# Storing K in one DRAM tensor so that a block is reloaded with its halo, putting one block's Q chunks ahead of its K chunks and moving one VectorE step earlier, in a two-layer attention and gated-MLP kernel

## The chip, the cores and the metric

The kernel runs on one core of one Trainium2 chip. The metric is device time in microseconds (us). The first three timed runs of the kernel before gave a median of 1631.23 us (1631.12 to 1631.37). Every execution also reports its span (first to last instruction), which is about 1.7 us shorter than its time, and the mean clock granted to TensorE. In the traces PE is TensorE's matmuls, PEld its weight loads, DVE VectorE, ACT ScalarE, POOL GpSimd, and SPq the SyncE queue, which issues nearly all DMAs (transfers), in program order. A DMA lands when its data has arrived. PSUM is the memory that TensorE writes its results to. Matmuls are called cold where the granted clock is low: a group of 8 takes 1.73 us at full clock.

## The reference

Two layers share one set of weights. Each is a sliding, dilated attention and a ReLU-gated MLP, each behind a layer norm and added to the residual. S = 2048 tokens, D = 1024, 32 heads of 32, MLP width 3584.

```python
qkv = (x @ wqkv).reshape(B, S, 3, H, Dh)          # ... split into q, k, v
idx = pos[:, None] - (arange(8) * 2)[None, :]     # 8 keys per query: 0, 2, ..., 14 tokens back
logits = einsum("bhsd,bhswd->bhsw", q, kg) * scale     # kg: k gathered at idx; -1e9 where idx < 0
o = einsum("bhsw,bhswd->bhsd", softmax(logits), vg)
x = x + o @ wo
gate, up = xn @ W_gate, xn @ W_up                 # xn = layernorm(x)
x = x + ((gate * (gate > 0)) * up) @ W_down
```

The keys of a query reach 14 tokens back. So a block of 512 tokens needs the last 14 K columns of the block before it: its halo.

## The kernel before

The tokens go through in four blocks of 512, twice (numbers 0 to 3 for layer one, 4 to 7 for layer two). TensorE makes V, Q, K, output projection, gate/up and down products; VectorE multiplies Q by the eight shifted Ks and sums over chunks (`t`, `ac`, `s`), and TensorE sums `s` over each head (`head_mm`, tile `L`). In layer one, Q and K of blocks 1 to 3 are made early, cast by ScalarE into a small staging pool (six buffers), stored to DRAM, and reloaded when VectorE gets to them. That is where the change is.

The halo was built on chip: each staged K chunk was widened by 14 columns that GpSimd copied in from the block before, and GpSimd saved its own last 14 columns for the block after.

```python
def f_(nm, c):                       # one chunk c of Q or K of block n: 8 matmuls, one cast
    def f():
        if nm == "k" and c == 0:
            khalo[n] = qk_pool.tile([P, KC, HALO], BF16, tag="kh", name=f"kh_{n}", bufs=2)
        ...                          # 8 matmuls into a PSUM buffer "acc" (six of them)
        else:
            k = tile_of("k", c, HALO + BLK)
            tail_act[0] = nc.scalar.copy(k[:, HALO:HALO + BLK], acc[:]).ins
            if b == 0:
                nc.gpsimd.memset(k[:, 0:HALO], 0.0)
            else:
                nc.gpsimd.tensor_copy(k[:, 0:HALO], khalo[n - 1][:, c, :])
            nc.gpsimd.tensor_copy(khalo[n][:, c, :], k[:, BLK:BLK + HALO])
    return f

QK_FIRST = [(nm, c) for c in range(KC) for nm in ("q", "k")]     # q0 k0 q1 k1 ...
```

The weights come in 1 MB slabs through a ring of five buffers; a slab's load is put into the queue at the time when a buffer should come free, and the author states when each slab was used last (`want_qk`: Q slabs, K slabs). The order of all instructions is fixed by a list of events with planned times, in units of `GRP` = 1.73 us, the time of one group of 8 matmuls:

```python
want_qk("qk01", t_v1, t_v1)          # both Q and K slabs of blocks 0 and 1 held until V of block 1 starts
want_v("v123", ...)                  # two V slabs; the second takes over a Q slab's buffer
...
qk1, puts1, gets1 = qk_steps(1, ln_a[1], "qk01", True)
ev.append((t_v2 + 2.2 * GRP, lambda: head_mm(0)))
...
spread(puts[ahead:], t_fill + GRP + 1.2, GRP)      # last K stores of blocks 2 and 3
spread(sums1[4:6], t_wo0 + 1.0, 6.0)               # products and sums of block 1
...
t_head1 = t_gu0 + 37.0
ev.append((t_head1, lambda: head_mm(1)))
ev.append((t_gu0 - 0.01, start_hidden))            # closes the staging pool, opens the MLP's hidden pool
```

`start_hidden` matters: the MLP's tiles (`r`, the ReLU of a gate, and `hT`) take over the memory of the staging pool. The first ReLU can therefore not start before the last staged K chunk has been read out by its store.

Of the kernel before, what the change touches and what calls it, by code (L numbers as in the profile page):

```python
# [7 lines left out]
BF16 = mybir.dt.bfloat16  # L8
# [5 lines left out]
P = 128  # L14
# [5 lines left out]
HALO = (W - 1) * DIL  # L20
KC = D // P
BLK = 512
# [14 lines left out]
def kernel(  # L37
# [11 lines left out]
    nc = tc.nc  # L49
    S = A_x.shape[1]  # L50
    F = B_W_gate.shape[1]
    assert A_x.shape[2] == D and S % BLK == 0 and F % P == 0
    NB = S // BLK
# [19 lines left out]
    dram = ctx.enter_context(tc.tile_pool(name="dram", bufs=1, space=bass.MemoryType.DRAM))  # L73
# [4 lines left out]
    qk_pool = ctx.enter_context(tc.tile_pool(name="qk", bufs=KC))  # L78
# [5 lines left out]
    pool = {}  # L84
# [25 lines left out]
    tail_act = [None]  # L110
# [4 lines left out]
    def sp_dma(dst, src, transpose=False):  # L115
        start = nc.sync.dma_start_transpose if transpose else nc.sync.dma_start
        if tail_sp[0] is None:
            tail_sp[0] = start(dst, src).ins
        else:
            with tc.issue_after(tail_sp[0]):  # L120
                tail_sp[0] = start(dst, src).ins  # L121

    @contextmanager
    def pe_group():
        if tail_pe[0] is None:
            yield
        else:
            with tc.issue_after(tail_pe[0]):
                yield

    def mm(*args, **kwargs):
        tail_pe[0] = nc.tensor.matmul(*args, **kwargs).ins  # L132
# [24 lines left out]
    NTOK = HALO + S  # L157
    v_d = dram.tile([H * DH, NTOK], BF16, name="v_d")
    o_d = dram.tile([NT, H, DH, P], BF16, name="o_d")
    q_d = [dram.tile([KC, P, BLK], BF16, name=f"q_d{n}") for n in range(1, NB)]  # L160
    k_d = [dram.tile([KC, P, HALO + BLK], BF16, name=f"k_d{n}") for n in range(1, NB)]
    s_d = [dram.tile([P, W * BLK], BF16, name=f"s_d{i}") for i in range(2)]
    zpad = const.tile([P, KC, HALO], BF16, name="zpad")
    nc.gpsimd.memset(zpad[:], 0.0)
# [22 lines left out]
    def want(key, src, use_end):  # L187
        slab_plan.append((key, src, use_end))

    def want_v(key, mid, end):  # L190
        for g in range(2):
            want((key, g), wqkv_v[:, :, 2 * D + g * SLAB:2 * D + (g + 1) * SLAB], mid if g == 0 else end)

    def want_qk(key, q_end, k_end):
        for i, (nm, end) in enumerate((("q", q_end), ("k", k_end))):
            for hh in range(2):
                want((key, nm, hh), wqkv_v[:, hh * (KC // 2):(hh + 1) * (KC // 2), i * D:(i + 1) * D], end)
# [242 lines left out]
    def store_v(n):  # L440
        def f():
            dst = bass.AP(tensor=v_d.tensor, offset=v_d.offset + HALO + (n % NB) * BLK,
                          ap=[[NTOK, P], [P * NTOK, KC], [1, BLK]])
            sp_dma(dst, att[n]["vT"][:])
        return f

    khalo = {}
# [8 lines left out]
    def qk_steps(n, ln, key, staged=False):  # L456
        b = n % NB
        st = att[n]
        staging = {}

        def tile_of(nm, c, cols):
            if staged:
                t = pool["stage"].tile([P, HALO + BLK], BF16, tag="st", name=f"{nm}st_{n}_{c}")
                staging[nm, c] = t[:, 0:cols]
                return t[:, 0:cols]
            t = qk_pool.tile([P, cols], BF16, tag=nm, name=f"{nm}_{n}_{c}")
            st[(nm, c)] = t
            return t[:]

        def f_(nm, c):  # L470
            def f():
                if nm == "k" and c == 0:
                    khalo[n] = qk_pool.tile([P, KC, HALO], BF16, tag="kh", name=f"kh_{n}", bufs=2)
                acc = psum.tile([P, BLK], F32, tag="acc", name=f"acc_{nm}")
                with pe_group():
                    for kc in range(KC):
                        w = slab[(key, nm, kc // (KC // 2))][:, kc % (KC // 2), bass.ds(c, P, KC)]
                        mm(acc[:], lhsT=w, rhs=ln["xnT"][:, :, kc, :], start=(kc == 0), stop=(kc == KC - 1))
                if nm == "q":
                    q = tile_of("q", c, BLK)  # L480
                    tail_act[0] = nc.scalar.copy(q, acc[:]).ins
                else:
                    k = tile_of("k", c, HALO + BLK)
                    tail_act[0] = nc.scalar.copy(k[:, HALO:HALO + BLK], acc[:]).ins  # L484
# [6 lines that stand above are left out]

        def put(nm, c):
            def f():
                sp_dma((q_d if nm == "q" else k_d)[n - 1][c], staging.pop((nm, c)))
            return f

        def get(nm, c):
            def f():
                t = qk_pool.tile([P, BLK if nm == "q" else HALO + BLK], BF16, tag=nm, name=f"{nm}_{n}_{c}")
                st[(nm, c)] = t  # L500
                sp_dma(t[:], (q_d if nm == "q" else k_d)[n - 1][c])
            return f

        order = QK_FIRST if n < NB else QK_ORDER
        steps = [f_(nm, c) for nm, c in order]
        if not staged:
            return steps
        return steps, [put(nm, c) for nm, c in order], [get(nm, c) for nm, c in order]

    def head_mm(n):  # L510
        st = att[n]
        st["L"] = psum_l.tile([P, W, P], F32, tag="L", name=f"L_{n}")
        with pe_group():
            for wh in range(2):
                for tq in range(TPB):
                    mm(st["L"][32 * tq:32 * tq + 32, WH * wh:WH * (wh + 1), :], lhsT=sel[:],
                       rhs=st["s"][:, WH * wh:WH * (wh + 1), tq * P:(tq + 1) * P],
                       start=True, stop=True, skip_group_check=True, tile_position=(0, 32 * tq))
# [281 lines left out]
    GRP = 1.73  # L800
# [4 lines left out]
    def spread(steps, at, gap):  # L805
        for i, f in enumerate(steps):
            ev.append((at + gap * i, f))

    ev = []
    ln_a = {}  # L810
# [6 lines left out]
    def ln1(n, at, turn_at, early=False, gap=3.0, dve=()):  # L817
        stats, apply, turn, hold = ln_steps(n, "a", early, dve)
        ln_a[n] = hold
        spread(stats, at, gap)  # L820
        spread(apply, at + (2 * gap if dve else max(3 * gap, 12.0)), gap)
        ev.append((turn_at, turn()))
# [15 lines left out]
    t_qk1 = t_qk0 + GRP * 2 * KC  # L838
    t_v1 = t_qk1 + GRP * 2 * KC
    t_v2 = t_v1 + GRP * KC  # L840
    t_v3 = t_v2 + GRP * KC
    t_qk2 = t_v3 + GRP * KC
    ahead = 2 * KC + 6
    t_wo0 = t_qk2 + GRP * ahead
# [1 line left out]
    t_gu0 = t_fill + GRP * (4 * KC - ahead)  # L846

    want_v("v0", t_v0 + GRP * 5, t_qk0)
    want_qk("qk01", t_v1, t_v1)
    want_v("v123", t_v3 + GRP * KC / 2, t_qk2)  # L850
    want_qk("qk23", t_qk2 + GRP * 2 * KC, t_gu0)
    want_wo(0, t_fill, t_fill)
# [10 lines left out]
    ev.append((t_qk0 + 4.0, store_v(0)))  # L863
    ev.append((t_qk0 + 18.0, lambda: load_x(3)))
    spread(qk_steps(0, ln_a[0], "qk01"), t_qk0, GRP)
    spread(prod_sum_steps(0), t_qk0 + 3.5, 4.4)
    spread(load_v_steps(0), t_qk0 + 19.0, 1.0)
    ln1(2, t_qk0 + 10.0, t_qk1 + 10.5, True, 4.5)
    qk1, puts1, gets1 = qk_steps(1, ln_a[1], "qk01", True)
    spread(qk1, t_qk1, GRP)  # L870
    spread(puts1, t_qk1 + GRP + 1.2, GRP)
    ln1(3, t_qk1 + 10.0, t_v2 + 0.4, True, 5.0)
    spread(v_steps(1, ln_a[1], "v123", True), t_v1, GRP)
# [9 lines left out]
    ev.append((t_v3 + 3.0, store_v(2)))  # L883
    spread(v_steps(3, ln_a[3], "v123", True), t_v3, GRP)
    ev.append((t_qk2 + 3.0, store_v(3)))
    spread(gets1, t_v3 + 4.0, 1.6)
    qk2, puts2, gets2 = qk_steps(2, ln_a[2], "qk23", True)
    qk3, puts3, gets3 = qk_steps(3, ln_a[3], "qk23", True)
    steps = qk2[0::2] + qk3[0::2] + qk2[1::2] + qk3[1::2]
# [7 lines left out]
    ln2(0, wo_ats, 3.0, [wo_ats[-1] + 1.0 + 1.3 * t for t in range(TPB)], (1, 2, 3))  # L897
    sums1 = prod_sum_steps(1)
    spread(sums1[:4], t_pv0 + 34.5, 4.5)
    spread(sums1[4:6], t_wo0 + 1.0, 6.0)  # L900
    spread(sums1[6:10], t_fill + 1.4, 4.6)
    spread(sums1[10:], t_gu0 + 2.6, 5.4)
    spread(load_v_steps(1), t_wo0 + 4.0, 7.0)
# [97 lines left out]
```

## Time and profile before

| | kernel before |
|---|---|
| time, first timed runs | 1631.23 us |
| the profiled execution: time, span | 1632.73 us, 1631.0 us |
| PE busy | 1612.0 us of the span |
| first wait of PE: V weights | 2.16 us at 87 us |
| second wait of PE: first ReLU | 7.36 us at 206 us |

The first line of the profile's page for the kernel before: busy time, share of the span and instructions of each engine.

```profile
PE 1612.0 (99%) x7513; PEld 784.8 (48%) x7562; DVE 1135.3 (70%) x961; ACT 476.5 (29%) x971; POOL 228.5 (14%) x212
```

TensorE leaves 19 us idle: 9.5 in the two waits above, 3.9 in the first 10 us of the program, 3.0 in its last 3 us, the rest in small pieces. Nothing can be won but what TensorE waits, and the slow matmuls that follow a wait. The table of waits of the kernel before (engine, what waited, for what: us in total, times, longest):

```profile
PE acc_g L132 <- ACT r L722: 7.4, 1, 7.4
...
DVE L L106 <- PE L L132: 3.4, 1, 3.4
...
PE acc_v L132 <- DMA w_v<-in_A_wqkv_dram: 3.0, 2, 2.2
```

The first line is the large stall, the last the small one (2.2 of its 3.0 us).

The small stall, from the timeline of the kernel before (start, duration, engine, line, operation, operands, count, and in brackets the idle time before it and what ended it):

```profile
80.00 7.07 PE L132 MATMUL acc_v<-xnT_a,w_v 128*128 128x512 bf16 x32
...
83.20 0.38 SPq L121 DMA_DIRECT2D w_v<-in_A_wqkv_dram  x1
...
89.23 5.96 PE L132 MATMUL acc_v<-xnT_a,w_v 128*128 128x512 bf16 x19 [2.16 <-DMA w_v<-in_A_wqkv_dram]
```

And from its chain of waits (start, duration, what):

```profile
80.05 2.21 POOL kst L488
...
82.28 0.32 SPq L121
```

The second V slab's buffer was free at 80.0, but the queue reached its load at 83.20, behind K stores that waited for GpSimd (its copy ended at 82.26, the store went at 82.28).

The large stall, from the same kernel's timeline:

```profile
194.51 8.05 SPq L121 DMA_DIRECT2D k_d<-kst  x4
...
196.03 0.59 ACT L484 CAST kst<-acc_k 128x512 bf16<-128x512 f32 x1 [0.91 <-DMA k_d<-kst]
...
199.88 4.48 DVE L106 TENSOR_TENSOR t<-q,k 128x2048 f32<-128x2048 bf16 x2
199.95 4.46 POOL L488 COPY kst<-kh 128x14 bf16<-128x14 bf16 x2
...
202.99 0.83 SPq L121 DMA_DIRECT2D w_u<-in_B_W_up_dram  x1
...
203.93 0.52 SPq L121 DMA_DIRECT2D w_g<-in_B_W_gate_dram  x1
...
204.55 1.66 SPq L121 DMA_DIRECT2D k_d<-kst  x1
...
212.41 1.57 ACT L722 ACTIVATE r<-acc_g 128x512 bf16<-128x512 f32 x3 [15.80 <-DMA k_d<-kst]
...
213.06 3.54 PE L132 MATMUL acc_g<-xnT_b,w_g 128*128 128x512 bf16 x8 [7.36 <-ACT r L722]
```

The last K chunk was cast by 196.6, but two GpSimd copies of 14 columns took 4.46 us, exactly beside two VectorE instructions of 4.48 us. The Trainium skill ("SBUF — State Buffer", section "SBUF: two separate sides") says that GpSimd and VectorE share a port pair into SBUF, the on-chip memory, as an exclusive lock, held for a whole instruction, and that a VectorE instruction with two inputs in SBUF, as these products have, contends for it with a GpSimd instruction that reads SBUF; this trace agrees: such a copy took 189 ns at its fastest and about 2.26 us beside VectorE's 2.28 us products. Only then could the store be issued, behind two 1 MB weight loads, and it landed about 8 us later. After it came the first ReLU.

Busy time of each engine in two stretches around the stalls, kernel before, with granted clock (PEclk), DMA share and GB/s:

```profile
80.00:100.00 20.00, 17.84 (x76) 7.56 (x75) 19.86 (x9) 12.06 (x26) 9.51 (x7) 0.91 0.70 244
200.00:225.00 25.00, 17.64 (x75) 7.58 (x74) 18.52 (x13) 3.37 (x6) 6.75 (x5) 0.86 0.56 180
```

Columns after the length: PE, PEld, DVE, ACT, POOL. A clock below 1.00 marks time at a lowered rate, which can begin during a wait (0.50 from 210 to 213 us, where no matmul ran) and goes on into the matmuls after it.

### The profile page before, as it was taken

The page shows a single profiled execution, that of the slowest core. Times are in us where ns is not written, and L with a number is a line of the kernel's source. Part 1 is how long each engine was busy: PE and PEld are TensorE (multiplying, and loading weights), DVE is VectorE, ACT ScalarE, POOL GpSimd, SP SyncE. Part 2 cuts the span into 40 slices and gives each one's busy share as a digit, 9 for nine tenths or more (in the row PEclk, how much of TensorE's full clock was granted, in tenths as well). Part 3 has the DMA queues.
Part 4 walks back from the last instruction along what each step waited for, and adds up shares of the span by engine and source line. Part 5 has one row for each costly group of instructions (what it writes and reads, how often), then busy time and mean ns, then how long its engine had stood idle before and what let it go on. Part 6 is the DMA issues. An engine that isn't in the chain of part 4 may idle for free.

```text
span 1631.0 us, 18776 instructions
## 1 busy us (share of the span) xinstructions
PE 1612.0 (99%) x7513; PEld 784.8 (48%) x7562; DVE 1135.3 (70%) x961; ACT 476.5 (29%) x971; POOL 228.5 (14%) x212
## 2 busy tenths in 40 slices
PE   9999989999999999999999999999999999999999
PEld 6646534444444445444454444544445444444444
DVE  6989889895979699939579295792948929311211
ACT  4843212041107222523135131360313301131110
POOL 2613500010003002210052000530005100000000
PEclk9999999999999999999999999999999999999999
DMA  9668756779579776785846948579585795655452
GB/s 294 139 207 250 174 168 197 209 186 241 185 208 212 174 216 190 200 222 166 232 159 186 229 154 230 181 184 251 167 225 161 204 251 162 207 156 179 155 162 71
DMA packets 401655, 315.87 MB, mean 194 GB/s; under 512 B 161056, under 2 KB 383648, under 8 KB 399904
## 3 DMA queue, kind: packets, MB, share of 16 engines
q1 hardware_dynamic: 400992, 314.09, 68.1%
q8 instruction: 59, 0.97, 0.3%
q10 hardware_dynamic: 576, 0.59, 0.1%
q14 instruction: 28, 0.23, 0.0%
HBM read 265.24 MB, written 33.67 MB: 183 GB/s over the span
## 4 chain that ended last, share of the span: by engine, by line
PE 97%; DMA 1%; issue 0%; POOL 0%; ACT 0%; SPq 0%; DVE 0%; DVEq 0%; ACTq 0%; POOLq 0%
PE acc_g L132 24%; PE acc_u L132 24%; PE dacc L132 18%; PE acc_wo L132 7%; PE acc_v L132 6%; PE acc_q L132 6%; PE acc_k L132 6%; PE dacc_pair L132 6%; DMA w_v<-in_A_wqkv_dram 1%; DMA k_d<-kst 1%; POOL st_a L249 0%; POOL kst L488 0%; SPq L121 0%; ACT xn_a L245 0%; PE L L132 0%
## 5 line engine op out<-in xcount | busy, mean ns | idle before, releaser
L132 PE MATMUL acc_g<-xnT_b,w_g 128*128 128x512 bf16 x1792 | 425.0, 380 | 7.4 <-ACT r L722 7.4
L132 PE MATMUL acc_u<-xnT_b,w_u 128*128 128x512 bf16 x1792 | 423.3, 379 | 0.0
L722 ACT ACTIVATE r<-acc_g 128x512 bf16<-128x512 f32 x224 | 133.4, 597 | 734.6 <-PE acc_g L132 663.0
L106 DVE TENSOR_TENSOR hT<-acc_u,r 128x512 bf16<-128x512 f32 x224 | 150.7, 686 | 245.6 <-PE acc_u L132 236.6
L132 PE MATMUL dacc<-w_d,hT 128*128 128x512 bf16 (+1 forms) x1372 | 300.4, 375 | 1.5
L132 PEld LDWEIGHTS <-w_g 128*128 128x128 bf16 x1792 | 175.6, 98 | 220.0 <-issue 9.7
L132 PEld LDWEIGHTS <-hT 128*128 128x128 bf16 x1820 | 178.1, 98 | 208.9
L132 PEld LDWEIGHTS <-w_u 128*128 128x128 bf16 x1792 | 175.4, 98 | 211.8 <-issue 0.5
L106 DVE TENSOR_TENSOR pv<-a,vhm 128x4096 bf16<-128x4096 bf16 x64 | 143.5, 2282 | 0.0
L541 DVE TENSOR_TENSOR t<-q,k 128x2048 f32<-128x2048 bf16 x56 | 128.0, 2291 | 6.7 <-ACT k L484 4.6
L769 DVE TENSOR_TENSOR x<-dacc,x 128x512 bf16<-128x512 f32 (+1 forms) x38 | 24.5, 672 | 154.2 <-PE dacc L132 154.2
L106 DVE TENSOR_TENSOR t<-q,k 128x2048 f32<-128x2048 bf16 x56 | 127.5, 2287 | 4.0 <-ACT k L484 2.4
L489 POOL COPY kh<-k 128x14 bf16<-128x14 bf16 x40 | 53.7, 1348 | 511.1 <-ACT k L484 511.1
L106 DVE TENSOR_TENSOR pv<-pv 128x1024 bf16<-128x1024 bf16 (+1 forms) x128 | 113.6, 948 | 0.0
L249 POOL TENSOR_TENSOR st_b<-st_b,neg_half 128x1 f32<-128x1 f32 x29 | 39.5, 1369 | 520.3 <-ACT st_b L248 520.3
L132 PE MATMUL acc_wo<-w_o,oT 128*128 128x512 bf16 x498 | 111.1, 379 | 0.7
L554 DVE TENSOR_TENSOR ac<-ac,t 128x2048 f32<-128x2048 f32 x48 | 109.6, 2283 | 0.3
L106 DVE TENSOR_TENSOR ac<-ac,t 128x2048 f32<-128x2048 f32 x48 | 109.6, 2283 | 0.0
L132 PE MATMUL dacc_pair<-w_d,hT 128*128 128x512 bf16 x413 | 95.5, 379 | 0.4
L132 PEld LDWEIGHTS <-oT 128*128 128x128 bf16 x512 | 50.0, 98 | 60.4
L244 ACT ACTIVATE xn_b<-x 128x1024 bf16<-128x1024 bf16 x29 | 30.3, 1046 | 124.2 <-DVE x L695 62.1
L410 ACT CAST vT<-acc_v 128x512 bf16<-128x512 f32 x56 | 32.7, 584 | 60.5 <-PE acc_v L132 60.5
(133 smaller groups left out, 1285.1 us busy)
## 6 DMA issues: line engine op xcount, KB each, us to landing
w_g<-in_B_W_gate_dram SPq DMA_DIRECT2D x56, 1024.0 KB, 6.7
w_u<-in_B_W_up_dram SPq DMA_DIRECT2D x56, 1024.0 KB, 5.3
w_d<-in_B_W_down_dram SPq DMA_DIRECT2D x48, 1024.0 KB, 5.9
w_o<-in_A_wo_dram SPq DMA_DIRECT2D x16, 1024.0 KB, 7.3
vhm<-v_d SPq DMA_DIRECT2D x32, 284.0 KB, 6.7
v_d<-vT SPq DMA_DIRECT2D x8, 1024.0 KB, 9.4
oT<-o_d SPq DMA_DIRECT2D x32, 256.0 KB, 4.2
w_d<-in_B_W_down_dram SPq DMA_DIRECT2D x16, 512.0 KB, 3.7
```

What stands on the lines that cost most here:

```text
L106: tail_dve[0] = f(*args, **kwargs).ins
L132: tail_pe[0] = nc.tensor.matmul(*args, **kwargs).ins
L244: nc.scalar.activation(xn, xt[:], ACT.Square, accum_out=sq)
L249: nc.gpsimd.tensor_tensor(rstd, vpe, neg_half[:, 0:1], op=ALU.pow)
L410: tail_act[0] = nc.scalar.copy(st["vT"][:, c, :], acc[:]).ins
L489: nc.gpsimd.tensor_copy(khalo[n][:, c, :], k[:, BLK:BLK + HALO])
L541: nc.vector.tensor_tensor(t[:], i0, i1, op=ALU.mult)
L554: nc.vector.tensor_tensor(o, ac[:], t[:], op=ALU.add)
L722: tail_act[0] = nc.scalar.activation(rs[j][:], acc[:], ACT.Relu).ins
L769: run = dv if n < NB - 2 else (lambda f, *args, **kwargs: f(*args, **kwargs))
```

## The change

K is stored once, without halo, into one DRAM tensor of all tokens, so that a block can be reloaded together with the 14 columns ahead of it: the widened read replaces 48 GpSimd copies. Block 0, which is never staged, keeps its copies, and one small store puts its last 14 columns into that tensor. For block 1 all Q chunks go ahead of all K chunks, so that the Q slabs come free 8 groups earlier. One step of block 1's products and sums moves 3.5 us earlier.

```diff
-    q_d = [dram.tile([KC, P, BLK], BF16, name=f"q_d{n}") for n in range(1, NB)]
-    k_d = [dram.tile([KC, P, HALO + BLK], BF16, name=f"k_d{n}") for n in range(1, NB)]
+    q_d = dram.tile([KC, P, S], BF16, name="q_d")
+    k_d = dram.tile([KC, P, S], BF16, name="k_d")
 ... (staging tiles are now 512 wide; khalo only where not staged)
+                elif staged:
+                    tail_act[0] = nc.scalar.copy(tile_of("k", c, BLK), acc[:]).ins
                 else:
                     k = tile_of("k", c, HALO + BLK)
 ... (put: stores to columns b*BLK to (b+1)*BLK)
 def get(nm, c):
-                sp_dma(t[:], (q_d if nm == "q" else k_d)[n - 1][c])
+                sp_dma(t[:], (q_d if nm == "q" else k_d)[c, :, b * BLK - lead:(b + 1) * BLK])   # lead: 14 for K
+    def store_halo(n):
+            end = (n % NB + 1) * BLK
+            sp_dma(k_d[:, :, end - HALO:end].rearrange("c p t -> p c t"), khalo[n][:])
 ...
-    want_qk("qk01", t_v1, t_v1)
+    want_qk("qk01", t_qk1 + GRP * KC, t_v1)
 ...
-    qk1, puts1, gets1 = qk_steps(1, ln_a[1], "qk01", True)
+    qk1, puts1, gets1 = (part[0::2] + part[1::2] for part in qk_steps(1, ln_a[1], "qk01", True))
+    ev.append((t_qk1 + 9.0, store_halo(0)))
 ... (block 1's reloads still alternate q and k)
-    spread(sums1[4:6], t_wo0 + 1.0, 6.0)
+    spread(sums1[4:6], t_wo0 + 1.0, 2.5)
```

More of the change, by code (lines that the diff above doesn't have):

```diff
@@ L462, in tile_of @@
             if staged:
-                t = pool["stage"].tile([P, HALO + BLK], BF16, tag="st", name=f"{nm}st_{n}_{c}")
-                staging[nm, c] = t[:, 0:cols]
-                return t[:, 0:cols]
+                staging[nm, c] = pool["stage"].tile([P, BLK], BF16, tag="st", name=f"{nm}st_{n}_{c}")
+                return staging[nm, c][:]
             t = qk_pool.tile([P, cols], BF16, tag=nm, name=f"{nm}_{n}_{c}")
@@ L471, in f @@
             def f():
-                if nm == "k" and c == 0:
+                if nm == "k" and c == 0 and not staged:
                     khalo[n] = qk_pool.tile([P, KC, HALO], BF16, tag="kh", name=f"kh_{n}", bufs=2)
@@ L493, in f @@
             def f():
-                sp_dma((q_d if nm == "q" else k_d)[n - 1][c], staging.pop((nm, c)))
+                sp_dma((q_d if nm == "q" else k_d)[c, :, b * BLK:(b + 1) * BLK], staging.pop((nm, c))[:])
             return f
@@ L498, in f @@
             def f():
-                t = qk_pool.tile([P, BLK if nm == "q" else HALO + BLK], BF16, tag=nm, name=f"{nm}_{n}_{c}")
+                lead = 0 if nm == "q" else HALO
+                t = qk_pool.tile([P, lead + BLK], BF16, tag=nm, name=f"{nm}_{n}_{c}")
                 st[(nm, c)] = t
-                sp_dma(t[:], (q_d if nm == "q" else k_d)[n - 1][c])
+                sp_dma(t[:], (q_d if nm == "q" else k_d)[c, :, b * BLK - lead:(b + 1) * BLK])
             return f
@@ L508, in qk_steps, with f @@
         return steps, [put(nm, c) for nm, c in order], [get(nm, c) for nm, c in order]
+    def store_halo(n):
+        def f():
+            end = (n % NB + 1) * BLK
+            sp_dma(k_d[:, :, end - HALO:end].rearrange("c p t -> p c t"), khalo[n][:])
+        return f
     def head_mm(n):
@@ L885 @@
     ev.append((t_qk2 + 3.0, store_v(3)))
-    spread(gets1, t_v3 + 4.0, 1.6)
+    spread([f for pair in zip(gets1[:KC], gets1[KC:]) for f in pair], t_v3 + 4.0, 1.6)
     qk2, puts2, gets2 = qk_steps(2, ln_a[2], "qk23", True)
```

## The prediction

> **What bounds the kernel.** TensorE: the page's busy table gives PE 1612.0 of 1631.0 us; the chain that ended last is 97% PE. The table of waits shows two stalls worth removing:
>
> 1. 87.07 to 89.23 us: value projection waits 2.16 us for the second slab of V weights. The timeline shows its load issued only at 83.20. Its slot in the ring comes free when the last K chunk of block 1 ends (80.0), and the issuing queue stood behind K stores waiting for GpSimd halo copies.
> 2. 205.70 to 213.06 us: six PSUM buffers are full because the first ReLU waits for the last K store to land (chain of waits: DMA k_d<-kst 7.71 us, then ACT r); the hidden-layer pool takes over the staging memory. That store was issued at 204.55, though its cast ended at 196.6. GpSimd copies of 14 columns took 189 ns when free but about 2.26 us, one DVE operation, when DVE was busy; the queue sat 194.51 to 202.56 in four K stores, and two weight loads of 1 MB went ahead of the last store.
>
> Each stall also chills TensorE[...]: 8 matmuls after stall 2 took 3.54 us where 1.73 is usual, +1.81; 19 after stall 1 took 5.96 against 4.10, +1.86. The windows show granted clock 0.84 and 0.91 there. Together 2.16 + 1.86 + 7.36 + 1.81 = 13.2 us. Start (about 10 us) and tail (about 3) are untouched.
>
> **What changes.** 48 GpSimd copies go (windows by tile: 58 us of GpSimd), so staged K stores wait for ACT alone. One store of 1024 pieces of 28 bytes comes; the like store of zeros landed in 8.3 us, and this one has tens of us before its first reader. With Q first, the Q slabs of block 1 free at about 66 us, so the V slab is issued some 17 us earlier and lands near 75, needed at 87. Moving one product/sum step 3.5 us earlier lets DVE fill about 2 us of idle time between the residual adds at 166 to 171 us.
>
> **On the critical path.** Stall 1 goes: -4.0 us. Stall 2: two weight loads and the last store can issue at about 195.5 to 196.8 (old time scale) instead of 202.99 to 204.55. First load to landing took 9.3 us, so the store lands near 204.8, the first ReLU ends near 205.4, and PE needs its buffer at 205.70. DVE, which ran to 206.56 before the first gate, is about 2 us earlier; the first up buffer is needed at 207.4. So the stall nearly closes, by a small margin: I give back 0.3 of 9.17. Sum 4.0 + 8.9 = 12.9; 1631.2 - 12.9 = 1618.3; with small new waits **1618.6 us**, range 1617.0 to 1622.5. Faster by over 2%: 0.005; within 2%: 0.985; slower: 0.01.
>
> **What would show it.** No PE wait for w_v; that slab's load issued near 66. No copies onto kst, GpSimd busy down about 58 us. Last K store issued about 9 us before the sixth gate/up group ends; PE wait for r from 7.4 to under 1 us. PE busy down about 3.7 us (no cold matmuls). No new PE wait.
>
> **What would make it wrong.** The last store lands 1 to 3 us later behind the weights: a short stall that brings back the cold 1.8 us (about 1621). Stores into one shared DRAM tensor ordered against reloads of other blocks, stalling the issuing queue. The small-piece store delaying Q stores until staging runs out. Early Q slab loads crowding stores and so ACT. DVE, with less slack in the first gate/up stage, holding PSUM.

## More of the kernel before

Note that the profiled execution was 1.5 us longer than the timed ones.

The head sums of block 0 in the kernel before, from the timeline:

```profile
103.11 0.61 PE L132 MATMUL L<-s,sel 128*32 128x512 bf16 x8
...
103.66 1.69 PE L132 MATMUL acc_v<-xnT_a,w_v 128*128 128x512 bf16 x7
103.78 0.27 DVE L106 TENSOR_TENSOR L<-L,maskc 32x112 f32<-32x112 f32 x1 [3.43 <-PE L L132]
```

VectorE had finished at 103.78 - 3.43 = 100.35, so TensorE, arriving at 103.11, found its data there with 2.8 us to spare. The head sums of block 1, from the same kernel's timeline:

```profile
239.97 2.29 DVE L106 TENSOR_TENSOR s<-ac,t 128x2048 bf16<-128x2048 f32 x1
...
242.43 0.61 PE L132 MATMUL L<-s,sel 128*32 128x512 bf16 x8
```

Here VectorE finished at 242.26, 0.17 us before TensorE came.

## The result, and the profile after

| | before | after |
|---|---|---|
| time, median (lowest to highest) | 1631.30 us (1631.12 to 1631.68) | 1622.68 us (1622.30 to 1623.05) |
| ratio of fast runs, 95% interval | | 0.9947 (0.9930 to 0.9964) |
| span of the profiled execution | 1631.0 us | 1620.6 us |
| PE waits for V weights at 87 us | 2.16 us | none |
| PE wait for the first ReLU | 7.36 us | 0.20 us |
| PE waits for `s` at the head sums | none | 0.84 and 1.14 us |

A ratio is the mean time of one kernel's fast runs over the mean of the other's in the same rounds, so it is not quite the ratio of the medians. The record marks an execution slow when it is over 1.5% above the fastest of the same kernel; none was. The change is 0.5% faster, 8.6 us; 12.6 were forecast (1631.2 to 1618.6), and 1622.68 lies just outside the forecast range (1617.0 to 1622.5).

Page of the kernel after, busy time:

```profile
PE 1609.6 (99%) x7513; PEld 784.4 (48%) x7562; DVE 1135.1 (70%) x961; ACT 475.8 (29%) x971; POOL 174.1 (11%) x164
```

48 GpSimd instructions and 54.4 us of its busy time are gone; PE is busy 2.4 us less for the same matmuls, where 3.7 were forecast: the windows from the V projection to block 0's head sums and from the first to the eighth gate/up group lost 1.86 and 1.62 us of busy time, but the first 20 us gained 0.62, and the two split head sums about 0.2 each. Table of PE's waits, kernel after:

```profile
PE L L132 <- DVE s L106: 2.0, 2, 1.1
...
PE acc_v L132 <- DMA w_v<-in_A_wqkv_dram: 1.0, 1, 1.0
...
PE acc_g L132 <- ACT r L730: 0.2, 1, 0.2
```

Both old stalls are gone (the w_v line that is left is at the start of the program, 10 us). In their place stands a wait that was not in the table of before: head sums wait for VectorE. The small stall, kernel after:

```profile
72.05 0.40 SPq L121 DMA_DIRECT2D w_v<-in_A_wqkv_dram  x1
...
80.08 19.16 PE L132 MATMUL acc_v<-xnT_a,w_v 128*128 128x512 bf16 x88
```

Now the slab's load is issued 11 us earlier, and 88 matmuls run without a gap. Timeline of the kernel after, at the hand-over from staging to hidden pool:

```profile
191.83 0.39 SPq L121 DMA_DIRECT2D w_u<-in_B_W_up_dram  x1
...
192.46 0.46 SPq L121 DMA_DIRECT2D w_g<-in_B_W_gate_dram  x1
...
192.51 0.59 ACT L482 CAST kst<-acc_k 128x512 bf16<-128x512 f32 x1 [1.14 <-PE acc_k L132]
193.12 2.93 SPq L121 DMA_DIRECT2D k_d<-kst  x1
...
202.34 1.57 ACT L730 ACTIVATE r<-acc_g 128x512 bf16<-128x512 f32 x3 [9.25 <-DMA k_d<-kst]
...
202.99 1.89 PE L132 MATMUL acc_g<-xnT_b,w_g 128*128 128x512 bf16 x8 [0.20 <-ACT r L730]
```

The store now follows its cast at once (193.12 against 192.51 + 0.59). It still takes 9 us to land, behind the weights, but the six PSUM buffers hide that to within 0.20 us.

The head sums of block 0, kernel after:

```profile
98.06 2.29 DVE L106 TENSOR_TENSOR s<-ac,t 128x2048 bf16<-128x2048 f32 x1
99.17 0.40 PE L132 MATMUL L<-s,sel 128*32 128x512 bf16 x4
...
100.41 0.40 PE L132 MATMUL L<-s,sel 128*32 128x512 bf16 x4 [0.84 <-DVE s L106]
...
100.74 1.47 PE L132 MATMUL acc_v<-xnT_a,w_v 128*128 128x512 bf16 x6
```

VectorE writes `s` at 98.06 to 100.35, to the hundredth where it did before. TensorE arrives 3.94 us earlier than before. The 2.8 us to spare have become a wait. The group took 100.74 - 99.17 = 1.57 us where before the next started after 103.66 - 103.11 = 0.55: 1.02 us lost. The head sums of block 1, kernel after:

```profile
229.90 2.29 DVE L106 TENSOR_TENSOR s<-ac,t 128x2048 bf16<-128x2048 f32 x1
...
230.70 0.40 PE L132 MATMUL L<-s,sel 128*32 128x512 bf16 x4
...
232.24 0.40 PE L132 MATMUL L<-s,sel 128*32 128x512 bf16 x4 [1.14 <-DVE s L106]
...
232.57 1.69 PE L132 MATMUL acc_g<-xnT_b,w_g 128*128 128x512 bf16 x7
```

Here the group took 232.57 - 230.70 = 1.87 us against 0.55: 1.32 us lost. The stretches shown of before, in the kernel after:

```profile
80.00:100.00 20.00, 19.57 (x94) 8.63 (x92) 19.86 (x9) 15.18 (x30) 1.63 (x2) 1.00 0.63 193
200.00:225.00 25.00, 24.80 (x116) 11.16 (x114) 23.39 (x17) 5.16 (x9) 0.00 (x0) 1.00 0.51 162
```

The clock is back at 1.00; VectorE's share of the second stretch rose from 18.5 to 23.4 us.

Added up from the starts of the same groups in both traces: the first gate group starts 2.92 us earlier (195.18 to 192.26), the eighth gate/up group 11.72 us earlier (216.43 to 204.71), so the large stall gave 8.80 us; the second head sums took 1.32 back; 11.72 - 1.32 = 10.4, the difference of the spans.

### The profile page after: what moved, and what is told of

Same layout as the page of the kernel before. It is cut to its first block, busy times and chain, and to the rows that moved or that the text cites. A ratio compares the mean times of both kernels' runs of the same rounds, so it can differ in the third digit from the quotient of the medians.

```text
span 1620.6 us, 18710 instructions
## 1 busy us (share of the span) xinstructions
PE 1609.6 (99%) x7513; PEld 784.4 (48%) x7562; DVE 1135.1 (70%) x961; ACT 475.8 (29%) x971; POOL 174.1 (11%) x164
## 4 chain that ended last, share of the span: by engine, by line
PE 93%; DVE 4%; DMA 1%; issue 1%; ACT 0%; SPq 0%; DVEq 0%; POOL 0%; ACTq 0%
PE acc_g L132 23%; PE acc_u L132 23%; PE dacc L132 18%; PE acc_wo L132 7%; PE acc_k L132 6%; PE acc_q L132 6%; PE acc_v L132 6%; PE dacc_pair L132 6%; DVE ac L106 2%; DVE t L106 2%; DMA k_d<-kst 1%; DMA w_v<-in_A_wqkv_dram 0%; DVE s L106 0%; DVE hT L106 0%; ACT xn_a L263 0%
```

## The experiments

Each was one kernel of before or after with an edit. All were correct. "Before" in a row is the kernel before, run in the same rounds on the same chip; its level differs by up to 1.6 us from chip to chip, so the ratios and the traces are compared. Times are medians.

| run | time | before | ratio (95%) | span of the profile | PE waits: V slab, ReLU, head sums |
|---|---|---|---|---|---|
| b_again | 1632.70 | 1632.84 | 1.0002 (0.9989 to 1.0015) | 1631.0 | 2.20, 7.66, none |
| b_kdram | 1625.55 | 1632.84 | 0.9960 (0.9948 to 0.9973) | 1623.8 | none, 2.93, 0.83 |
| b_qfirst | 1630.41 | 1632.84 | 0.9988 (0.9975 to 1.0002) | 1628.6 | none, 8.08, 0.87 |
| b_put | 1625.75 | 1632.84 | 0.9958 (0.9946 to 0.9971) | 1624.4 | 2.44, 2.29, none |
| after_again | 1622.14 | 1631.25 | 0.9943 (0.9930 to 0.9955) | 1620.4 | none, none, 0.83 + 1.14 |
| a_noq | 1622.24 | 1631.25 | 0.9942 (0.9930 to 0.9955) | 1620.7 | none, 0.9, 0.82 + 1.14 |
| a_sums | 1625.15 | 1632.24 | 0.9961 (0.9947 to 0.9975) | 1623.7 | none, 2.99, 0.82 |
| a_put | 1620.55 | 1631.25 | 0.9933 (0.9920 to 0.9945) | 1618.9 | none, none, 0.83 |
| a_head01 | 1620.08 | 1631.25 | 0.9931 (0.9917 to 0.9944) | 1617.9 | none, none, none |
| a_best | 1619.37 | 1632.24 | 0.9922 (0.9910 to 0.9935) | 1617.3 | none, none, none |

By the 2% rule every one counts as "same" as before; the intervals, and the waits above all, are what tells them apart.

The theory after the result: the two stalls went as forecast, and the missing gain is in two places: 2.3 us of new waits at the head sums, and about 1.5 us that were never there in the timed runs, because the profile was of a longer execution. Rivals: that the profile itself lengthens an execution; that VectorE limits the whole stage, so that moving a wait moves nothing; and, on the parts of the change, that the order of Q and K is what did it.

### The kernel before, unchanged (b_again, b_look1, b_look2)

> The kernel before, unchanged. The prediction took 13.2 us of stall from one profile whose execution took 1632.73 us, 1.5 us more than the 1631.2 us of the timed ones. Theory A (the profile on record caught longer stalls than usual): timed spans near 1629.6, and a second profile shows the wait before acc_v below 2.16 us or the wait before acc_g below 7.36 us, together 1 to 2 us less idle or cold time on TensorE. Rival B (profiling itself adds 1.5 us to any execution): the second profile is again near 1631.0 of span with the same two waits, and the timed spans of this run are near 1629.6 all the same.

Its profile has span 1631.0 again with the same two waits, but so had its timed runs (1630.6 to 1632.5), and profiled and unprofiled ones mix. So rival B falls: profiling adds nothing that shows. The kernel before just scatters: in all its runs here, spans from 1628.6 to 1633.0. Theory A's means, a shorter wait, was not seen either. What differs showed in two more looks.

> The kernel before, unchanged, one more profile. Both profiles so far have span 1631.0 and cold matmuls after stall 1; many timed executions have span 1629.1 to 1629.5. Theory (the same 2.2 us stall leaves TensorE cold in some executions only): in an execution with span under 1630 the 2.2 us wait before acc_v is still there, but the matmuls after it run at full rate (19 in about 4.1 us, not 5.96). Rival (the short executions have a shorter stall): the wait is under 1 us in such a one.

> The same again, as which of the two kinds an execution is can't be chosen: the same two readings are expected.

Timeline of PE in b_look1 (span 1632.9):

```profile
88.95 13.95 PE L132 MATMUL acc_v<-xnT_a,w_v 128*128 128x512 bf16 x56 [1.99 <-DMA w_v<-in_A_wqkv_dram]
...
213.65 3.57 PE L132 MATMUL acc_g<-xnT_b,w_g 128*128 128x512 bf16 x8 [8.23 <-ACT r L722]
217.02 3.14 PE L132 MATMUL acc_u<-xnT_b,w_u 128*128 128x512 bf16 x8
```

and in b_look2 (span 1631.0):

```profile
89.42 12.26 PE L132 MATMUL acc_v<-xnT_a,w_v 128*128 128x512 bf16 x56 [2.21 <-DMA w_v<-in_A_wqkv_dram]
...
212.15 3.57 PE L132 MATMUL acc_g<-xnT_b,w_g 128*128 128x512 bf16 x8 [7.94 <-ACT r L722]
215.52 2.75 PE L132 MATMUL acc_u<-xnT_b,w_u 128*128 128x512 bf16 x8
```

After nearly the same wait, 2.0 and 2.2 us, 56 matmuls took 13.95 us in one execution and 12.26 in the other (full rate is 12.1). After the large wait the second group took 3.14, 2.75 or, in the first profile, 1.90 us. In the four profiles of this kernel the small wait varies by 0.2 us and the large one by 0.9 (7.36 to 8.23), the cold time after them by 1.7 and 1.25. So what varies most is how long TensorE stays cold after a wait, not the wait. Part of the expectation was not met: no look fell into an execution with a span under 1630. That those are the ones with full rate after the small stall and a short cold stretch after the large one (1631.0 - 1.8 = 1629.2) is worked out, not shown. The record gives it some support: the executions in the rounds of the experiments list their mean granted clock, and of those of the kernel before the ones with spans up to 1629.7 show 0.998, those from 1630.1 to 1631.6 show 0.997, and those from 1632.5 up 0.996. A thousandth of the span is 1.6 us.

### Each part alone (b_kdram, b_qfirst, a_noq, a_sums)

b_kdram: the changed kernel with the order of Q and K, the slab plan and the product/sum step put back.

```diff
-    want_qk("qk01", t_qk1 + GRP * KC, t_v1)
+    want_qk("qk01", t_v1, t_v1)
-    qk1, puts1, gets1 = (part[0::2] + part[1::2] for part in qk_steps(1, ln_a[1], "qk01", True))
+    qk1, puts1, gets1 = qk_steps(1, ln_a[1], "qk01", True)
 ... (block 1's reloads in the old order too)
-    spread(sums1[4:6], t_wo0 + 1.0, 2.5)
+    spread(sums1[4:6], t_wo0 + 1.0, 6.0)
```

> K kept in DRAM with its halo reloaded, no GpSimd copies, but Q and K chunks of block 1 alternate as before, the slab plan and the product/sum spacing are those of before. Theory (the GpSimd copies alone held up both the last K store and the load of the V slab): the V slab is issued near 80.2 instead of 83.2 and lands near 87, so stall 1 falls below 0.5 us; the wait for r falls from 7.4 to 0 to 2 us; time 1622 to 1625. Rival (the order of Q and K carries stall 1 alone): stall 1 stays near 2 us with its cold matmuls, time 1626 to 1628.

The small stall is gone with the order untouched: the V slab was issued at 79.79. The theory holds there, the rival falls. On the large stall the theory was too hopeful: 2.93 us stayed, where at most 2 were expected, with cold matmuls after it, and the time, 1625.55, is above the 1622 to 1625 expected. The timeline of the queue in b_kdram shows why:

```profile
188.16 1.28 SPq L121 DMA_TRANSPOSE xnT_b<-xn_b  x1
...
195.39 1.58 SPq L121 DMA_DIRECT2D k_d<-kst  x1
```

The queue stood until 188.16 for VectorE's last normalised tile, then had eight DMAs and the two weight loads to issue, and the last store left 2.3 us later than in the kernel after, where that transpose left at 185.72.

b_qfirst: the kernel before with the Q-first lines of the diff alone.

> The kernel before with only block 1's Q chunks ahead of its K chunks and the earlier release of the Q slabs; GpSimd copies kept. Theory: stall 1 (2.16 us and 1.86 us cold) goes, but TensorE then reaches the head sums of block 0 before VectorE has its sums, near 99.2 against 100.4, so about 1 us comes back as a wait there; stall 2 stays at 7 us or more: time 1627.5 to 1628.5. If the head sums did not wait, it would be 1627.2; if the copies delay the queue as much as the order did, stall 1 stays and time is 1631.

The small stall goes here too, and the wait at the head sums appears (0.87), as the theory says. But 0.4 us more than in b_again is lost at the large stall, and the time, 1630.41, is above the 1628.5 expected, partly because before stood at 1632.84 on this chip. Against b_again, by the starts of the groups, 4.1 us are won at 87 us, 1.0 of them is given back at the head sums and 0.6 at the large stall; 2.4 are left, the difference of the spans.

a_noq: the changed kernel with the order of Q and K put back (the first two pairs of lines above, and the reload order).

> The changed kernel with block 1's Q and K chunks alternating again and the Q slabs released as before; K in DRAM and the earlier product/sum step kept. Theory (K in DRAM alone already ends stall 1, so the order adds nothing once the copies are gone; the earlier product/sum step is what closes the rest of stall 2 by letting the last normalised tile, and with it the queue's K stores, go 2.5 us earlier): within 0.8 us of the changed kernel, wait for r under 0.6 us. Rival (the Q order is what closes the rest of stall 2 through earlier slab loads): like the run with K in DRAM alone, a wait for r of about 2.9 us and a span 3 us longer.

The theory holds: the same time as the changed kernel in the same rounds (1622.24 and 1622.14). Its wait for the ReLU (0.9 us) is above the 0.6 expected, but small beside the 2.9 of b_kdram; its V projection also started 0.6 us earlier than in after_again (79.53 and 80.12), which may be why. Once the copies are gone, the order of Q and K is worth nothing that shows.

a_sums: the changed kernel with the product/sum step put back (6.0 for 2.5).

> The changed kernel with only the product/sum step of block 1 back at its old place (6.0 instead of 2.5 us after the one ahead of it); K in DRAM and Q first kept. Theory (that step, and not the Q order, closes the rest of stall 2): as the run with K in DRAM alone, a last K store issued near 2.8 us after the first gate group starts instead of 0.9, a wait for r of 2.5 to 3.2 us with cold matmuls after it, no wait at the head sums of block 1, span 1623 to 1625. Rival (Q first makes up for it): within 0.8 us of the changed kernel.

The theory holds, the rival falls: wait 2.99 us, no wait at block 1's head sums, span 1623.7, the same as b_kdram. So this one number is worth 3 us, and by a way the prediction did not have: the prediction thought of VectorE reaching its first gate in time; in the traces the step lets VectorE start the last normalised tile 2.3 us earlier (185.15 against 187.44), and with it the queue that carries the K stores.

### The last store ahead of the weights (b_put, a_put)

The same edit to the kernel before and to the changed one:

```diff
-    spread(puts[ahead:], t_fill + GRP + 1.2, GRP)
+    spread(puts[ahead:-1], t_fill + GRP + 1.2, GRP)
+    ev.append((t_gu0 + 0.2, puts[-1]))      # ahead of the two slab loads at t_gu0 + 0.3
```

> The kernel before with one event moved: the last K store is queued ahead of the two 1 MB weight loads that follow it, not behind. GpSimd copies kept. The store can still be issued only when GpSimd is done, near 204.5. Theory (stall 2 is two delays in series, GpSimd lateness of about 8 us and about 5.5 us behind the weights, and the PSUM buffers hide 8 to 9 us of them): it now lands about 2.3 us after issue, near 206.5, so the wait for r falls from 7.4 to 1 to 2 us and time to 1624 to 1626. Rival (GpSimd lateness is all of it): it lands as late as before, near 210 to 212, and time stays 1630 to 1631.

The theory holds. From the chain of waits of b_put:

```profile
198.47 4.42 POOL kst L488 x2
...
202.90 2.75 DMA k_d<-kst
```

GpSimd is as late as ever, but the store lands in 2.75 us rather than about 8, and the wait falls from 7.66 to 2.29 us (1 to 2 were expected). The Trainium skill ("DMA: Bandwidth & Descriptors", section "Queues, rings and completion order") says that each DMA engine consumes one queue's descriptors in order; this agrees with it. So the large stall was two delays in series, about 8 us of GpSimd (cast done at 196.6, store issued at 204.55) and about 5 us behind the weights (7.71 less 2.75), and the PSUM buffers could hide most of one of them but not both: 2.29 us of wait are left with GpSimd's delay alone, 0.20 to 2.99 with the weights' alone (after, b_kdram, a_sums). One moved line, with GpSimd left as it was, won 0.42%. Not all of that is the store's: the wait fell by 5.4 us, over half of the 8.6 us that the whole change won, but in this profile also the small stall (2.44 us) left no cold matmuls (56 in 12.26 us, against 13.95 in b_again), which the moved store does not explain.

> The changed kernel with only the last K store queued ahead of the two weight loads. It lands near 195.5 instead of 202.1, so the wait for r (0.2 us) goes and VectorE no longer idles 1.6 us before the first gate. Theory (VectorE's delay at the staging hand-over is what makes it late for the head sums of block 1): the wait there falls from 1.1 us to 0.3 or less, span falls by 1.0 to 1.5 us, while the wait of block 0, 40 us earlier, stays at 0.8. Rival (block 1's head sums wait for VectorE's total work, not for this delay): the wait stays and span falls by 0.2 us.

The theory holds: no wait for the ReLU, none at block 1's head sums, 0.83 still at block 0's; the mean of its runs is 1.58 us below the changed kernel's in the same rounds (1620.48 and 1622.06), a little more than the 1.0 to 1.5 expected.

### The head sums later (after_again, a_head01, a_best)

> The changed kernel, unchanged, beside the kernel before and the variants below on one chip. Spans of 1620 to 1621.5 as in its first runs; ratio to before 0.9935 to 0.995. Theory A (before varies between executions because a 2 us stall sometimes leaves TensorE cold and sometimes not, and the changed kernel has no stall of that length): its executions agree within 1 us while those of before scatter over 2 us. Rival: both scatter alike.

Its runs lie within 0.83 us (1621.71 to 1622.54), those of before in the same rounds over 1.69 (1630.89 to 1632.58), with no clock below 1.0 in any of its runs. That agrees with theory A in kind, though the scatter of before is under the 2 us expected and is taken over nine runs against five. In b_kdram and a_sums, where about 3 us of wait for the ReLU were left, one execution each lay 2.8 to 2.9 us above the median, at a lower clock (0.998 against 0.999).

a_head01:

```diff
-    ev.append((t_v2 + 2.2 * GRP, lambda: head_mm(0)))
-    spread(softmax_steps(0), t_v2 + 2.3 * GRP, 0.01)
+    ev.append((t_v2 + 3.2 * GRP, lambda: head_mm(0)))
+    spread(softmax_steps(0), t_v2 + 3.3 * GRP, 0.01)
-    ev.append((t_head1, lambda: head_mm(1)))
-    spread(softmax_steps(1), t_head1 + 0.1, 3.5)
+    ev.append((t_head1 + 2.0, lambda: head_mm(1)))
+    spread(softmax_steps(1), t_head1 + 2.1, 3.5)
```

> The changed kernel with only the head sums moved: those of block 0 one value-projection group later (1.73 us), those of block 1 one gate/up pair later (3.45 us). Theory (the missing 2.3 us are TensorE reaching the head sums before VectorE has written its products' sums: 1.0 us in block 0, 1.3 us in block 1): both waits for s vanish, span falls by 2.0 to 2.4 us, to about 1618.4. Rival (VectorE is the limit of the whole stage, so a wait moved away comes back at the next point where TensorE needs it, a gate or the reloaded attention output): span falls by under 0.7 us and a new wait of 1 us or more shows.

The whole table of PE's waits in a_head01:

```profile
PE scratch L132 <- DVE ones L290: 1.5, 1, 1.5
PE acc_v L132 <- DMA w_v<-in_A_wqkv_dram: 0.9, 1, 0.9
PE tp L358 <- DVE mean L106: 0.4, 1, 0.4
```

All three are in the first 10 us of the program. The mean of its runs is 2.05 us below the changed kernel's (1620.02 and 1622.06), which is the size of the new waits. The theory holds, and the rival falls: VectorE was not late for anything else.

a_best has both edits, to the head sums and to the last store.

> The changed kernel with both mends: head sums moved later, last K store ahead of the weight loads. Theory (after moving the head sums no wait of TensorE is left but those of the start, so the earlier store has nothing more to give): within 0.5 us of the run with only the head sums moved, 0.7% faster than before. Rival (the two add up): another 1 to 1.5 us faster, span near 1616.8.

The theory holds in the main: no wait is left but at the start. Its span is 0.6 us below a_head01's, a little more than the 0.5 expected; but its V projection of block 1 already started 0.6 us earlier (79.55 against 80.16), and so does that of other kernels in some executions, so this part is put down to the start. The ratios alone (0.9931 and 0.9922, with overlapping intervals) do not rule out the 1 to 1.5 us of the rival; that no wait is left in either trace speaks against it. At 1619.37 us, 0.78% below before, it is the fastest version here. It beats the change by 0.2%, with intervals of the two that overlap across chips.

## Why the prediction was right or wrong

| term | predicted | in the two profiles |
|---|---|---|
| small stall and its cold matmuls | -4.0 us | -3.94 us |
| large stall and its cold matmuls | -8.9 us | -8.80 us |
| head sums of block 0 | 0 | +1.02 us |
| head sums of block 1 | 0 | +1.32 us |
| small new waits | +0.3 us | none else |
| sum, of spans | -12.6 us | -10.4 us |
| longer execution in the profile than in the timed runs | not allowed for | 1632.73 - 1631.3 = 1.4 us that the timed runs did not have to give |
| time | 1618.6 us | 1622.68 us |

(-3.94 is the shift at block 0's head sums, 103.11 to 99.17.) The 0.4 us still missing between 10.4 and the measured 8.6 is on the other side: the profiled execution of the kernel after, 1622.30 us, was its fastest, against a median of 1622.68.

- Right: what bounds the kernel, the two stalls, their causes and their sizes. The store was forecast to land near 204.8 on the old time scale; it landed at 202.12, which with the 2.92 us shift is 205.0. The wait for the ReLU fell to 0.20 us. GpSimd's busy time fell by 54 us (58 forecast). The small pieces and the shared DRAM tensor caused no wait: the store of 28-byte pieces landed in 3.9 us.
- Wrong, the step that failed: "No new PE wait." The prediction followed what the stalls held up and never asked what had been using them. VectorE had 2.8 us to spare at block 0's head sums and about 0.2 at block 1's; 4 us were taken out ahead of the first, and by the second TensorE had moved 11.73 us earlier (242.43 to 230.70) but VectorE only 10.07 (`s` ended at 242.26 and 232.19). a_head01 shows the cost, 2.05 us in time. The wait of VectorE for `L`, 3.4 us in the table of waits of before, had announced it at block 0; at block 1 no wait in the table did, and the margin of 0.17 us had to be read from the timeline.
- Wrong, a mis-sized term: the sum of 13.2 us was read off one execution of 1632.73 us and taken from a median of 1631.2. In the repeats the wait lengths barely moved, but the cold stretch after them ran from nothing to 1.8 us (small stall) and from 1.65 to 2.9 us (large stall, by the starts of the groups). That the 1.4 us which the timed runs did not have was cold time is inferred from this and from the clocks of the timed runs; no profile of a short execution shows it. The predicted 1.81 us after the large stall was also a little high: it compares a busy time (3.54 us, with its overlap into the next group) with a spacing; by the starts it is 1.65.
- Right in effect, wrong in its reason: the Q order was credited with the small stall. It does end it alone (b_qfirst), but so does K in DRAM (b_kdram), and beside that it adds nothing (a_noq). The slab was issued at 72.05, not near 66, as the queue had a transpose ahead of it; it made no difference.
- Right in effect, wrong in its way: the moved product/sum step. It closed the last 3 us of the large stall (a_sums), through the queue and not through VectorE's first gate.

## What to carry to other kernels

When a stall of the bottleneck engine is to be removed, list the other engines' waits for that engine downstream of it, and at the other places where it takes their data the margin between the two: each is slack that the stall was paying for, and where it was smaller than the stall here, most of the difference came back as a new wait (1.0 and 1.3 us). A stall at the end of an in-order queue can be two delays in series behind one buffer depth, so look for the cheaper one: here one moved store took 5.4 us off the large stall, where the restructuring won 8.6 us in all. And take stall sizes from several executions, or at least from one whose time is that of the timed runs.

## What the Trainium skill lacked or had wrong

- "TensorE: Matmul & The Clock Gate", Part 1 and its section on HAM oscillation: it puts the fall to half rate at idle gaps of a window of about 3.4 us or more. Here waits of 1.99 to 2.20 us for the V slab were followed by cold matmuls in three profiles (56 matmuls in 13.95 us, 12.1 being full rate), and so were waits of 2.29 to 2.99 us for the ReLU in three more (b_put, b_kdram, a_sums: 1.7 us lost by the starts of the groups), while waits of 2.21 and 2.44 us for the V slab in two others were not (12.26 us). So a gap shorter than the page's window can cost 1.7 to 1.8 us more; what decides it is not shown. In the first profile the clock was still 1.00 when the wait ended at 89.23, and 0.50 from about 90.2 to 93.5. Waits of 0.8 to 1.1 us never did this.
- The same page says not to fit to a count of cold matmuls, as the window runs freely; the runs agree and give the size for a single long wait: 7.4 to 8.2 us of waiting cost another 1.65 to 2.9 us.
- "SBUF — State Buffer" has the port lock, with a figure for a DMA that GpSimd issues, but none for a small GpSimd instruction beside a busy VectorE: 14 columns took 0.19 us alone and 2.26 us beside products of 2.28 us, and four stores that waited for such copies held the queue for 8.05 us.
- "DMA: Bandwidth & Descriptors" gives at least 512 bytes for line rate, but no whole cost for a small scattered store: 1024 pieces of 28 bytes landed in 3.9 us and delayed nothing that shows.
